# Attention beside an MLP on one core: the value product always runs beside the next quad's scores, across batches; the first MLP stage follows one quad behind; spare score banks serve two flushes

## Chip, cores and metric

The kernel runs on one core of a Trainium2 chip. The metric is the device time of one execution in microseconds (us), lower is better. Before the change it was 466.85 us (median of 3 runs, 465.77 to 469.23). Engine names are those of the profile: PE (TensorE), PEld (its weight loads), DVE (VectorE), ACT (ScalarE), POOL (GpSimd), SP (SyncE, which issues most DMAs).

## The reference

Attention with a forgetting gate over 8 batches, 8 heads, 576 positions and head size 64, then an MLP with tanh-GELU over the 4608 tokens (512 to 2048 to 512):

```python
def _attn_ref(q, k, v, f):
    scores = (1.0 / np.sqrt(D)) * np.matmul(q, k.transpose(0, 1, 3, 2))
    cum = np.cumsum(np.log(np.clip(f, 0.0001, 1.0)), axis=-1)
    decay = cum[:, :, :, None] - cum[:, :, None, :]
    scores = np.where(causal, -1000000000.0, scores + decay)
    ...                                    # softmax over the last axis
    return np.matmul(attn, v)

def _moe_ref(x, w_in, w_out):              # x: (B*S, H*D)
    h = x @ w_in
    return gelu_tanh(h) @ w_out
```

## The kernel before

Heads go in quads of four, two quads to a batch, 16 in all. For a quad:

- the scores come in four rounds, 48 matmuls with 32 rows each in all (8 or 16 a round); two ACT exponentials per round read them from two tiles of the score pool `psS` (two tiles of two PSUM banks each) and write `pt`;
- DVE multiplies the diagonal blocks of `pt` by a triangle, the **masks**; the strips are t = 0 to 4, and the last score round makes those of t = 2 and t = 4;
- the **value product** of one head is seven matmuls into `po` (two banks, a single buffer). Its columns 256 to 831 hold the numerators on one half of the partitions and the denominators on the other. An ACT copy (`num`) and a DVE transpose (`den`) read it. After two heads come a reciprocal, a second transpose (`rb`), and a **POOL multiply** that writes `xT`, the MLP's input;
- POOL also makes `v_aug`, the values times the gate's weight, the product's stationary operand.

The first MLP stage of a batch (`mlp_in`: 128 matmuls into `psS` tiles, 16 GELUs on ACT) needs `xT` of both quads. The second (`mlp_out`) is a generator: `pull(fill, n)` takes n of its 512-column matmuls as filler between other work.

```python
    def attn_out(i, h):                                   # value product of head h of quad i
        po = psO.tile([128, 1024], FP32, name="po", tag="po")
        p, va = pt[i % 2], v_aug[i % 2]
        for t in (0, 1, 3, 2, 4):
            for (a, z, base) in po_parts:
                ...                                       # matmuls into po
        ...
        nc.scalar.copy(num[mine, :], po[mine, 256:256 + S])
        nc.vector.transpose(out=den[mine, :], in_=po[other, 256:256 + S])
        if y == 1:                                        # second head of a pair
            ...                                           # rec = 1 / den; rb = rec, transposed
            nc.gpsimd.tensor_mul(xT[b % 2][:, 2 * u + x, :], num, rb)

    def step(i, j, fill, per_round, n=None):              # scores of quad i, products of quad j
        for r in range(4):
            if i is not None:
                score_round(i, r)
                ...
            if j is not None:
                attn_out(j, r)
            if r == 0:
                ...
                if i is not None:
                    make_vaug(i)
            ...                                           # r 1, 2: transposes of k, q of quad n
            if i is not None and r > 0:
                mask(i, r - 1)
            pull(fill, per_round)
            if i is not None and r == 3:
                mask(i, 3)

    # the loop over batches, from batch 1 on
            elif b + 1 < B:
                i = QPB * (b + 1)
                extra = b % 2
                pull(fill, 3)
                step(i, None, fill, 5 + 2 * extra)        # scores, no products
                step(i + 1, i, fill, 5 + extra)           # both
                step(None, i + 1, fill, 3)                # products, no scores: a flush
                pull(fill, 5)
```

The softmax here doesn't subtract the row's maximum and nothing guards it: scores larger than these inputs give would overflow.

Of the kernel before, what the change touches and what calls it, by code (L numbers as in the profile page):

```python
# [8 lines left out]
FP32 = mybir.dt.float32  # L9
# [7 lines left out]
def kernel(  # L17
# [10 lines left out]
    nc = tc.nc  # L28

    B, H, S, D = q.shape  # L30
# [10 lines left out]
    NQ = BH // 4  # L41
    QPB = H // 4
# [22 lines left out]
    psS = ctx.enter_context(tc.tile_pool(name="psS", bufs=2, space=bass.MemoryType.PSUM))  # L65
    psO = ctx.enter_context(tc.tile_pool(name="psO", bufs=1, space=bass.MemoryType.PSUM))
# [30 lines left out]
    def load_heads(src, dst, i, eng):  # L97
        b, h0 = i // QPB, 4 * (i % QPB)

        return [eng.dma_start(  # L100
            out=dst[i % 2][32 * h:32 * h + 32].rearrange("p a e d -> p a (e d)"),
            in_=src[b, h0 + h].rearrange("(a p e) d -> p a (e d)", p=32, e=2),
        ) for h in range(4)]

    def load_qk(i):
        return load_heads(k, k_nat, i, nc.sync) + load_heads(q, q_nat, i, nc.sync)
# [6 lines left out]
    def load_v(b, h0=0, nh=H):  # L113
        ins = []
        for t in range(NT):
            n = min(128, S - 128 * t)
            ins.append(nc.sync.dma_start(
                out=v_nat[b % 2][:n, t, h0:h0 + nh, :],
                in_=v[b, h0:h0 + nh, 128 * t:128 * t + n, :].rearrange("h p d -> p h d"),
            ))  # L120
        return ins
# [24 lines left out]
    def cast_k(i):  # L146
        nc.gpsimd.tensor_copy(k_bf, k_nat[i % 2])

    def cast_q(i):
        nc.gpsimd.tensor_copy(q_bf, q_nat[i % 2])  # L150

    def transpose_k(i):
        transpose_one(k_bf, kT[i % 2])
# [46 lines left out]

    pair = [None, None]

    def attn_out(i, h):
        po = psO.tile([128, 1024], FP32, name="po", tag="po")
        p, va = pt[i % 2], v_aug[i % 2]

        for t in (0, 1, 3, 2, 4):
            for (a, z, base) in po_parts:
                s = max(a, 128 * t)
                if s >= z:  # L210
                    continue
                nc.tensor.matmul(  # L212
                    po[:, base + s - a:base + z - a],
                    va[:, t, h, :],
                    p[:, h, strip_off[t] + s - 128 * t:strip_off[t] + z - 128 * t],
                    start=(t == 0), stop=(t == (1 if z == 256 else 4)),
                    skip_group_check=True,
                )
        b, u, x, y = i // QPB, i % QPB, h // 2, h % 2
        if y == 0:  # L220
            pair[0] = num_pool.tile([128, S], FP32, name="num", tag="num")
            pair[1] = den_pool.tile([128, S], FP32, name="den", tag="den")
        num, den = pair
        mine, other = slice(64 * y, 64 * y + 64), slice(64 - 64 * y, 128 - 64 * y)
        nc.scalar.copy(num[mine, :], po[mine, 256:256 + S])  # L225
        nc.vector.transpose(out=den[mine, :], in_=po[other, 256:256 + S])  # L226
        if y == 1:

            rec = den_pool.tile([128, S // 32], FP32, name="rec", tag="rec")
            nc.vector.reciprocal(rec, den[:, 0:S:32])  # L230
            rb = den_pool.tile([128, S], FP32, name="rb", tag="rb")
            nc.vector.transpose(out=rb.rearrange("p (c j) -> p c j", j=32),  # L232
                                in_=rec.unsqueeze(2).to_broadcast([128, S // 32, 32]))
            nc.gpsimd.tensor_mul(xT[b % 2][:, 2 * u + x, :], num, rb)  # L234


    def mlp_in(b, fts):

        hS = S // 2
        tiles = [psS.tile([128, 2, 512], FP32, name="ps_h", tag="s") for _ in fts]  # L240
        for dts in (range(N_DT - 1), range(N_DT - 1, N_DT)):
            for ft, ph in zip(fts, tiles):
                for dt in dts:
                    for j in range(2):
                        nc.tensor.matmul(  # L245
                            ph[:, j, 0:hS],
                            w_in_sb[:, dt, 128 * ft:128 * ft + 128],
                            xT[b % 2][:, dt, hS * j:hS * (j + 1)],
                            start=(dt == 0), stop=(dt == N_DT - 1),
                        )  # L250
        o = S * (b % 2)
        for ft, ph in zip(fts, tiles):
            nc.scalar.activation(  # L253
                gT[:, ft, o:o + S].rearrange("p (j n) -> p j n", j=2),
                ph[:, :, 0:hS], AF.Gelu_apprx_tanh)
# [63 lines left out]
    def make_w():  # L319
        cum_ps = psM.tile([128, NT * BH], FP32, name="cum_ps", tag="m")  # L320
        nc.tensor.matmul(cum_ps, utri_f32, logfT, start=True, stop=False)
        nc.tensor.matmul(cum_ps[:, BH:], ones_f32, before, start=False, stop=True)
        for (rows, t0, t1) in ((128, 0, NT - 1), (LAST, NT - 1, NT)):
            nc.scalar.activation(
                wT[:rows, :, t0:t1, :].rearrange("p i t h -> p t i h"),
                cum_ps[:rows, t0 * BH:t1 * BH].rearrange("p (t i h) -> p t i h", i=NQ, h=4),
                AF.Exp, scale=-1.0, bias=shift[:rows, :])


    def pull(it, n):  # L330
        for _ in range(n):
            if next(it, False) is False:
                return
# [4 lines left out]
    def step(i, j, fill, per_round, n=None):  # L338
# [5 lines that stand above are left out]
                if i == 0 and r == 0:  # L344
                    make_w()
            if j is not None:
                attn_out(j, r)
            if r == 0:
                if n is not None:
                    cast_k(n)  # L350
                    cast_q(n)
                if i == 0:
                    w_in_dmas.append(load_w_in(0))
                if i is not None:
                    make_vaug(i)
            if n is not None:
                if r == 1:
                    transpose_k(n)
                if r == 2:
                    transpose_q(n)  # L360
# [6 lines that stand above are left out]
    def prepare_one(i):  # L367
        cast_k(i)
        transpose_k(i)
        cast_q(i)  # L370
        transpose_q(i)

    def prepare(b):

        for i in range(b * QPB, b * QPB + QPB):
            prepare_one(i)
            if i + QPB < NQ:
                load_qk(i + QPB)
        if b + 1 < B:
            load_v(b + 1)  # L380

    with tc.manual_schedule():
        setup()
        step(0, None, none, 0, n=1)
        w_in_dmas.extend(load_w_in(c) for c in range(1, 4))
        qk2 = load_qk(2)
        after(qk2[0], w_in_dmas[2])
        step(1, 0, none, 0)
        w_out_dmas = [load_w_out(c) for c in range(2)]
        v1 = load_v(1)  # L390
        after(v1[0], w_out_dmas[0])
        load_qk(3)
        step(None, 1, none, 0)
        fill = none
        for b in range(B):
            mlp_in(b, (0, 1))
            for x in fill:
                pass
            if b == 0:
                prepare_one(2)  # L400
                for c in range(2, 4):
                    load_w_out(c)
            elif b + 1 < B:
                prepare(b + 1)
            for ft in range(2, N_FT):
                mlp_in(b, (ft,))
            fill = mlp_out(out_tiles(b))
            if b == 0:
                step(2, None, fill, 9, n=3)
                load_qk(4)  # L410
                step(3, 2, fill, 4)
                load_qk(5)
                load_v(2)
                step(None, 3, fill, 1)
                pull(fill, 4)
            elif b + 1 < B:
                i = QPB * (b + 1)
                extra = b % 2
                pull(fill, 3)
                step(i, None, fill, 5 + 2 * extra)  # L420
                step(i + 1, i, fill, 5 + extra)
                step(None, i + 1, fill, 3)
                pull(fill, 5)
        for x in fill:
            pass

# [1 line left out]
_INS = ['q', 'k', 'v', 'f', 'moe_w_in', 'moe_w_out']  # L428
# [26 lines left out]
```

## Time and profile before

The page of the kernel before, parts 1 and 2 (busy time as a share of the span; busy tenths in 40 equal slices):

```profile
PE 373.1 (80%) x2789; PEld 216.9 (47%) x2825; DVE 180.3 (39%) x295; ACT 244.5 (53%) x340; POOL 130.0 (28%) x127
PE   1654699858997799967998799967998699968996
```

No engine is full on average. The row of PE shows where: it reaches 9 in every batch, in the first MLP stage, and falls to 6 to 8 in between. Two batches as windows (start to end of the stretch, its length, busy time of each engine with the number of its instructions, granted PE clock, DMA share and rate):

```profile
core 0: us, PE busy (x) PEld busy (x) DVE busy (x) ACT busy (x) POOL busy (x), PEclk, DMA share, GB/s
219.10:272.60 53.50, 46.14 (x357) 26.85 (x361) 21.27 (x35) 30.44 (x43) 16.14 (x15) 0.97 0.44 92
272.60:324.70 52.10, 43.22 (x340) 25.57 (x344) 20.46 (x34) 29.92 (x42) 14.64 (x14) 0.97 0.41 89
```

A batch took 52 to 53.5 us, and PE stood still for 7 to 9 us of it. Who waited for whom (total us, times, longest):

```profile
DVE den L226 <- ACT num L225: 82.8, 61, 2.2
PE po L212 <- DVE den L226: 37.3, 50, 1.6
PE po L212 <- DVE pt_95 L198: 16.5, 16, 1.1
```

Products waited 37.3 us for the transpose that frees `po`, and the transpose waited for the copy. The timeline where the mixed step meets the flush (start, duration, engine, line, operation, count, and in brackets the idle time before it and what ended that):

```profile
360.76 0.78 DVE L232 STREAM_TRANSPOSE rb<-rec 128x576 f32<-128x576 f32 x1
361.46 2.13 DVE L198 TENSOR_TENSOR pt_95<-pt_95,utri 128x512 bf16<-128x512 bf16 x3
361.69 1.42 POOL L234 TENSOR_TENSOR xT_96<-num,rb 128x576 bf16<-128x576 f32 x1 [4.24 <-DVE rb L232]
361.90 0.43 PE L212 MATMUL po<-pt_95,v_aug_93 128*128 128x128 bf16 x3 [1.01 <-DVE pt_95 L198]
363.44 0.39 PE L212 MATMUL po<-pt_95,v_aug_93 128*128 128x320 bf16 x2 [1.11 <-DVE pt_95 L198]
...
363.93 0.63 ACT L225 COPY num<-po 64x576 f32<-64x576 f32 x1 [4.31 <-PE po L212]
364.59 0.78 DVE L226 STREAM_TRANSPOSE den<-po 64x576 f32<-64x576 f32 x1 [1.00 <-ACT num L225]
365.43 1.49 PE L212 MATMUL po<-pt_95,v_aug_93 128*128 128x256 bf16 x7 [0.31 <-DVE den L226]
```

In the flush a product, a copy and a transpose follow one another (363.44 to 365.37), and only then may the next product start.

### The profile page before, as it was taken

What the parts mean: (1) busy time and instruction counts of PE and PEld (TensorE: products, weight loads), DVE (VectorE), ACT (ScalarE), POOL (GpSimd) and SP (SyncE); (2) the same over time, 40 slices, a digit from 0 to 9 for tenths busy, and PEclk for the clock granted to TensorE, in tenths of its full rate; (3) what the DMA queues carried; (4) which work ended last, traced back from release to release, by engine and by line L of the source; (5) the groups of instructions that cost most, each with busy time, mean ns of one, the idle gap of its engine ahead of it and who ended that gap; (6) DMA issues with size and microseconds to landing.
All of it is one profiled execution on the core that took longest, in us unless ns stands there. A gap on an engine that the chain in (4) does not pass through costs nothing.

```text
span 465.6 us, 6954 instructions
## 1 busy us (share of the span) xinstructions
PE 373.1 (80%) x2789; PEld 216.9 (47%) x2825; DVE 180.3 (39%) x295; ACT 244.5 (53%) x340; POOL 130.0 (28%) x127
## 2 busy tenths in 40 slices
PE   1654699858997799967998799967998699968996
PEld 0222374425743465434734366434744366434752
DVE  5474412464127530455126530365215540364011
ACT  2733357714675347733676247743677247743610
POOL 1443380115502181024601272024601262022000
PEclk9999999967999899989999899999999899998999
DMA  9996980592941059000971049100961010000011
GB/s 189 146 193 111 201 146 24 124 196 63 227 94 45 24 127 200 24 23 34 207 134 47 23 108 210 34 24 24 226 125 46 2 44 1 24 23 23 24 46 68
DMA packets 86016, 42.55 MB, mean 91 GB/s; under 512 B 40352, under 2 KB 81312, under 8 KB 85984
## 3 DMA queue, kind: packets, MB, share of 16 engines
q1 hardware_dynamic: 79328, 36.73, 36.2%
q0 software_dynamic: 4224, 4.19, 5.8%
q10 hardware_dynamic: 2432, 1.18, 1.3%
q8 instruction: 22, 0.36, 0.3%
q14 instruction: 10, 0.08, 0.1%
HBM read 36.85 MB, written 9.44 MB: 99 GB/s over the span
## 4 chain that ended last, share of the span: by engine, by line
PE 53%; DVE 18%; ACT 15%; issue 6%; DMA 3%; POOL 2%; POOLq 0%; SPq 0%; ACTq 0%; DVEq 0%
PE ps_h L245 25%; PE pso L263 14%; PE po L212 10%; DVE den L226 9%; ACT num L225 7%; PE ps_s L180 4%; ACT pt_94 L189 4%; DVE pt_95 L198 3%; ACT pt_95 L189 3%; DVE rb L232 3%; DVE pt_94 L198 2%; POOL xT_96 L234 1%; DMA k_nat_82<-in_k_dram 1%; DMA k_nat_83<-in_k_dram 1%; DMA q_nat_81<-in_q_dram 1%
## 5 line engine op out<-in xcount | busy, mean ns | idle before, releaser
L263 PE MATMUL pso<-w_out_sb,gT 128*128 128x512 bf16 x540 | 140.2, 391 | 1.9 <-issue 0.6
L245 PEld LDWEIGHTS <-w_in_sb 128*128 128x128 bf16 x1024 | 101.7, 99 | 39.8 <-issue 10.5
L253 ACT ACTIVATE gT<-ps_h 128x576 bf16<-128x576 f32 x128 | 82.4, 650 | 66.9 <-PE ps_h L245 66.9
L225 ACT COPY num<-po 64x576 f32<-64x576 f32 x64 | 40.4, 632 | 93.8 <-PE po L212 93.3
L226 DVE STREAM_TRANSPOSE den<-po 64x576 f32<-64x576 f32 x64 | 49.9, 780 | 83.0 <-ACT num L225 82.8
L263 PEld LDWEIGHTS <-gT 128*128 128x128 bf16 x576 | 51.6, 100 | 57.5 <-issue 9.2
L212 PE MATMUL po<-pt_95,v_aug_93 128*128 128x320 bf16 (+4 forms) x224 | 39.0, 316 | 43.1 <-DVE den L226 26.5
L245 PE MATMUL ps_h<-xT_96,w_in_sb 128*128 128x288 bf16 x512 | 67.6, 293 | 5.0 <-POOL xT_96 L234 4.6
L245 PE MATMUL ps_h<-xT_97,w_in_sb 128*128 128x288 bf16 x512 | 65.4, 288 | 3.2 <-POOL xT_97 L234 3.2
L198 DVE TENSOR_TENSOR pt_94<-pt_94,utri 128x512 bf16<-128x512 bf16 (+1 forms) x40 | 21.8, 565 | 111.3 <-ACT pt_94 L189 110.9
L234 POOL TENSOR_TENSOR xT_97<-num,rb 128x576 bf16<-128x576 f32 x16 | 22.6, 1412 | 144.4 <-DVE rb L232 144.4
L234 POOL TENSOR_TENSOR xT_96<-num,rb 128x576 bf16<-128x576 f32 x16 | 22.6, 1410 | 129.5 <-DVE rb L232 119.0
L189 ACT ACTIVATE pt_95<-ps_s 128x800 bf16<-128x800 f32 (+3 forms) x64 | 50.1, 834 | 15.6 <-PE ps_s L180 15.2
L189 ACT ACTIVATE pt_94<-ps_s 128x800 bf16<-128x800 f32 (+3 forms) x64 | 50.1, 834 | 14.5 <-PE ps_s L180 14.4
L212 PEld LDWEIGHTS <-v_aug_93 128*128 128x128 bf16 x224 | 24.3, 115 | 65.0 <-issue 56.8
L267 DVE COPY o_st<-pso 128x512 f32<-128x512 f32 x36 | 24.8, 688 | 63.2 <-PE pso L263 62.9
L212 PE MATMUL po<-pt_94,v_aug_92 128*128 128x320 bf16 (+4 forms) x224 | 30.2, 276 | 15.9 <-DVE den L226 10.8
L180 PE MATMUL ps_s<-qT_88,kT_90 32*128 32x400 bf16 (+5 forms) x384 | 25.2, 295 | 12.2 <-ACT pt_94 L189 6.6
L212 PEld LDWEIGHTS <-v_aug_92 128*128 128x128 bf16 x224 | 20.1, 101 | 27.2 <-issue 20.4
L232 DVE STREAM_TRANSPOSE rb<-rec 128x576 f32<-128x576 f32 x32 | 24.9, 778 | 2.2
L180 PEld LDWEIGHTS <-kT_90 32*128 32x128 bf16 x384 | 10.1, 95 | 30.9 <-issue 24.8
L198 DVE TENSOR_TENSOR pt_95<-pt_95,utri 128x512 bf16<-128x512 bf16 (+1 forms) x40 | 23.1, 609 | 0.0
(55 smaller groups left out, 184.9 us busy)
## 6 DMA issues: line engine op xcount, KB each, us to landing
out_dram<-o_st SPq DMA_DIRECT2D x36, 256.0 KB, 2.0
k_nat_82<-in_k_dram SPq DMA_DIRECT2D x32, 144.0 KB, 3.1
k_nat_83<-in_k_dram SPq DMA_DIRECT2D x32, 144.0 KB, 4.4
v_nat_87<-in_v_dram SPq DMA_DIRECT2D x16, 256.0 KB, 5.8
q_nat_80<-in_q_dram SPq DMA_DIRECT2D x28, 144.0 KB, 3.8
q_nat_81<-in_q_dram SPq DMA_DIRECT2D x28, 144.0 KB, 5.0
v_nat_86<-in_v_dram SPq DMA_DIRECT2D x12, 256.0 KB, 5.9
w_in_sb<-in_moe_w_in_dram POOLq DMA_DIRECT2D x4, 512.0 KB, 6.3
```

The lines of the kernel that those rows point to most:

```text
L180: nc.tensor.matmul(tiles[h // 2][:, h % 2, c0:c0 + nq], kk[32 * h:32 * h + 32, 128 * t:128 * t + 128, c], qq[32 * h:32 * h + 32, q0:q0 + n ...
L189: nc.scalar.activation(p[:, 2 * g:2 * g + 2, off:off + n], tiles[g][:, :, 0:n], AF.Exp, scale=scale)
L198: nc.vector.tensor_mul(p[:, :, o:o + w], p[:, :, o:o + w], utri[:, :, :w].to_broadcast([128, 4, w]))
L212: nc.tensor.matmul(po[:, base + s - a:base + z - a], va[:, t, h, :], p[:, h, strip_off[t] + s - 128 * t:strip_off[t] + z - 128 * t], start ...
L225: nc.scalar.copy(num[mine, :], po[mine, 256:256 + S])
L226: nc.vector.transpose(out=den[mine, :], in_=po[other, 256:256 + S])
L232: nc.vector.transpose(out=rb.rearrange("p (c j) -> p c j", j=32), in_=rec.unsqueeze(2).to_broadcast([128, S // 32, 32]))
L234: nc.gpsimd.tensor_mul(xT[b % 2][:, 2 * u + x, :], num, rb)
L245: nc.tensor.matmul(ph[:, j, 0:hS], w_in_sb[:, dt, 128 * ft:128 * ft + 128], xT[b % 2][:, dt, hS * j:hS * (j + 1)], start=(dt == 0), stop=( ...
L253: nc.scalar.activation(gT[:, ft, o:o + S].rearrange("p (j n) -> p j n", j=2), ph[:, :, 0:hS], AF.Gelu_apprx_tanh)
L263: nc.tensor.matmul(pso, gT[:, ft, c:c + 128], w_out_sb[:, ft, :], start=(ft == 0), stop=(ft == N_FT - 1))
L267: nc.vector.tensor_copy(st, pso)
```

## The change

The intent is that, once the pipeline is filled, no product runs without scores beside it, and no scores without a product (quads 0 and 2 still make their scores alone). The pipeline of quads therefore runs on across batches. The first MLP stage of batch b starts when the products of its second quad are done, and by then the scores of the next batch's first quad are made already. Only quad 1 (nothing else to run yet) and the last quad still have a flush; there every second product goes to a bank pair of the score pool, which nothing else uses then. The transpose is put ahead of the copy.

```diff
-    def attn_out(i, h):
-        po = psO.tile([128, 1024], FP32, name="po", tag="po")
+    def attn_out(i, h, spare=False):
+        if spare:
+            po = psS.tile([128, 2, 512], FP32, name="ps_o", tag="s").rearrange("p a n -> p (a n)")
+        else:
+            po = psO.tile([128, 1024], FP32, name="po", tag="po")
...
+        nc.vector.transpose(out=den[mine, :], in_=po[other, 256:256 + S])
         nc.scalar.copy(num[mine, :], po[mine, 256:256 + S])
-        nc.vector.transpose(out=den[mine, :], in_=po[other, 256:256 + S])
...
-                attn_out(j, r)
+                attn_out(j, r, spare=(i is None and r % 2 == 1))
...                                    # batch 0: step(2, None, 7), step(3, 2, 4), step(4, 3, 3)
             elif b + 1 < B:
-                i = QPB * (b + 1)
-                extra = b % 2
+                i = 2 * b + 3
+                per_round = 7 + 2 * (b % 2)
                 pull(fill, 3)
-                step(i, None, fill, 5 + 2 * extra)
-                step(i + 1, i, fill, 5 + extra)
-                step(None, i + 1, fill, 3)
-                pull(fill, 5)
+                step(i, i - 1, fill, per_round)
+                if i + 1 < NQ:
+                    step(i + 1, i, fill, per_round)
+                else:
+                    step(None, i, fill, 5)
+                    pull(fill, 6)
```

Casts, transposes and loads of q, k and v move with the quads (cut here).

## The prediction

> **What bounds it now.** The page's first part shows PE busy 80% of 465.6 us, ACT 53%, DVE 39%. Stretches by stage show about 53 us per batch: 14 us of first MLP stage with PE full, then 38 us of attention filled with the second MLP stage, PE busy 28 to 31. The chain of waits ends 16% of the span in the DVE transpose and ACT copy of `po`. The timeline of one batch (338 to 378 us) splits the 38: four rounds with scores and filler but no value product, 9.5 us (2.4 each: the two exponentials take 1.5 to 1.7 and the next scores wait for them); four with both, 11.5 us; a flush of four without scores, 11.3 us, where each product (0.7 us of issue warm, 1.5 cold) waits for the copy (0.63) then transpose (0.78) of the one before. Value products waited 37 us in all for transposes.
>
> **The change, costed.** Matmul counts stay. Two full steps replace empty step, full step and flush in batches 1 to 5. From the mixed rounds: scores 0.51, product 0.69, six fillers 1.39 us (0.22 each plus 0.1 for switching). So a round with 7 fillers is about 2.82 us, with 9 about 3.28. ACT needs 2.3 of it (two exponentials, one copy), DVE under 2.5 on average: PE should bind. In rounds 1 and 3 of the old mixed step the product waited 0.4 to 0.6 us, since the copy stands behind two exponentials and the transpose behind the copy. Transposing first lets it run beside the exponentials; the pair still takes 1.4 us serially (the Trainium skill, PSUM — Partial Sum Buffer, "PSUM bank collisions raise a hardware error", has different quadrants harmless, but the trace shows every transpose after its copy), so a bare flush gains only by the spare banks.
>
> Steady batch: first stage with its tail 17.2 us (its wait for the last `xT` falls from 1.1 to under 0.5), steps 23.5 or 27.1: 41 and 44 us, not 53.
>
> **Sum (spans).**
> - Flush of quad 1 (42.6 to 52): products back to back, 5.5 us saved.
> - Batch 0: steps 10.2 + 9 + 9 us (the last two bound by ACT); first stage of batch 1 starts near 96, not 109.7, with quad 4's scores made.
> - Batches 1 to 5: 46 + 40.5 + 44.5 + 40.5 + 44.5 = 216, giving 312.
> - Batch 6: 29 to its step's end, flush 7.5, pull 1.4: 350.
> - Batch 7: 38.5 as before.
> That is 388, plus 1.5 (span to time), plus 3 for small waits: 393 us.
>
> PE's clock should gain: the Trainium skill (TensorE: Matmul & The Clock Gate, Part 1) has an idle array throttled to half clock; here flush products took 1.49 us against 0.86 in full rounds, and the granted clock was 0.83 to 0.96 in attention stages, 1.00 in the MLP stage.
>
> **What would show it.** Products waiting for transposes under 10 us; PE about 90% busy; rounds of 2.8 and 3.3 us; periods alternating 41 and 44; granted clock 0.98 or more.
>
> **What would make it wrong.** The copy, waiting for the transpose in ACT's queue, holds up the exponentials when DVE is late (masks take 0.38 to 0.71 us); rounds then stretch to 3.2 to 3.6. Earlier loads compete with `w_out` near 55 to 75 us. The last `xT` chain (3.6 us) may stand exposed at each batch.

## The result and the profile after

The kernel after took 406.39 us (median of 4 runs, 405.86 to 407.24), against 466.31 us for the kernel before (4 runs). The ratio is 0.8707, 95% interval 0.8665 to 0.8749. Ratios in this document are the mean time of one kernel's fast runs over that of the other's of the same rounds, so not quite the ratio of the medians quoted. So 60 us were saved where 73 were forecast: the time is 13 us above the 393 us of the prediction.

The same parts of the page, after:

```profile
PE 354.4 (88%) x2825; PEld 209.4 (52%) x2825; DVE 199.2 (49%) x295; ACT 244.2 (60%) x340; POOL 135.0 (33%) x127
PE   0546699959899899979999899979999999989996
```

PE does the same work in a shorter span and is now 88% busy. DVE's busy time **rose** from 180.3 to 199.2 us with the same 295 instructions. The masks, 80 of them, account for it: they took 44.9 us in the trace before and 65.7 us in the trace after. Two batches, with the columns as before:

```profile
195.40:241.00 45.60, 43.61 (x361) 25.94 (x360) 23.37 (x35) 30.18 (x43) 16.09 (x15) 1.00 0.48 107
241.00:284.20 43.20, 40.48 (x345) 24.50 (x344) 23.35 (x34) 30.23 (x43) 16.11 (x15) 1.00 0.53 107
```

A batch takes 45.6 and 43.2 us in place of 53.5 and 52.1. PE still stands still for 2 to 2.7 us of it. The waits:

```profile
DVE den L228 <- PE po L215: 124.2, 53, 13.7
PE po L215 <- DVE pt_95 L198: 14.1, 16, 1.1
PE po L215 <- ACT num L229: 5.9, 9, 1.6
```

The transpose now waits for the product itself, not for the copy. A product waits 5.9 us in all for what frees its bank (37.3 before). The wait for the masks `pt_95` hardly moved: 14.1 us for 16.5. It stands in one place per batch, the **joint** where the first step meets the second:

```profile
175.09 0.78 DVE L228 STREAM_TRANSPOSE den<-po 64x576 f32<-64x576 f32 x1 [1.64 <-PE po L215]
...
176.20 0.78 DVE L235 STREAM_TRANSPOSE rb<-rec 128x576 f32<-128x576 f32 x1
176.90 3.20 DVE L198 TENSOR_TENSOR pt_95<-pt_95,utri 128x512 bf16<-128x512 bf16 x3
176.96 0.81 PE L215 MATMUL po<-pt_95,v_aug_93 128*128 128x256 bf16 x5
...
177.12 1.43 POOL L237 TENSOR_TENSOR xT_97<-num,rb 128x576 bf16<-128x576 f32 x1 [4.13 <-DVE rb L235]
178.51 2.71 POOL L164 TENSOR_TENSOR v_aug_92<-v_nat_86,wT 128x640 bf16<-128x640 f32 x2
178.88 0.30 PE L215 MATMUL po<-pt_95,v_aug_93 128*128 128x320 bf16 x1 [1.11 <-DVE pt_95 L198]
180.15 0.19 PE L215 MATMUL po<-pt_95,v_aug_93 128*128 128x64 bf16 x1 [0.97 <-DVE pt_95 L198]
```

PE has the scores and five matmuls of the product behind it at 177.8 and then waits for two masks. The three masks at 176.90 take 0.38, 1.62 and 1.35 us. The second begins at 177.21, just after POOL's multiply began (177.12), and ends 0.28 us after it (178.83 after 178.55). The third stands against POOL's next instruction, the first half of `v_aug`, in the same way (180.10 after 179.95).

The Trainium skill (SBUF — State Buffer, "Who interferes with whom") states this: "A DVE instruction with two SBUF inputs contends with a GpSimd instruction that reads SBUF", and the one that comes second blocks. The trace agrees. A mask has two inputs in SBUF and takes 0.38 to 0.43 us where no POOL instruction runs beside it; the transposes of `po` have one input, in PSUM, and take 0.78 us with or without a POOL multiply beside them. Both pieces of POOL's work at the joint, the multiply into `xT` and `v_aug`, read SBUF.

The second of them was not at this place before. A `v_aug` buffer comes free when its quad's products end. Before, both buffers were free after the flush, and POOL made both during the MLP stage (in the trace before, at 328.5 and 331.1 us, far from any mask). After, one buffer still serves the running pipeline, and the second `v_aug` of a batch can only be made when the first step's products are done, which is the joint.

To count, here are the seven distances between the starts of the eight score rounds of a batch, for two batches, worked out from the start of each round's first score matmul in the trace. The fifth is the joint; the eighth round is not in it, since the MLP stage follows:

```
                    9 fillers a round                     7 fillers a round
predicted           3.28 in each                          2.82 in each
kernel after        3.35 3.17 3.24 3.18 5.30 3.17 3.24    2.92 2.92 2.81 2.75 5.29 2.74 2.81
```

Six of the seven distances lie within 0.11 us of the forecast. The joint costs 2.1 or 2.5 us more than the rounds beside it.

### The profile page after: what moved, and what is told of

Read it like the earlier page. It is cut to its first block, busy times and chain, and to the rows that moved or that the text cites. A ratio compares the mean times of both kernels' runs of the same rounds, so it can differ in the third digit from the quotient of the medians.

```text
span 404.6 us, 6926 instructions
## 1 busy us (share of the span) xinstructions
PE 354.4 (88%) x2825; PEld 209.4 (52%) x2825; DVE 199.2 (49%) x295; ACT 244.2 (60%) x340; POOL 135.0 (33%) x127
## 3 DMA queue, kind: packets, MB, share of 16 engines
q10 hardware_dynamic: 2432, 1.18, 1.4%
## 4 chain that ended last, share of the span: by engine, by line
PE 71%; DVE 17%; DMA 4%; POOL 3%; ACT 3%; issue 2%; SPq 0%; POOLq 0%; DVEq 0%; ACTq 0%
PE ps_h L248 29%; PE pso L266 25%; PE po L215 11%; PE ps_s L180 6%; DVE pt_95 L198 5%; DVE den L228 4%; DVE rb L235 3%; DVE pt_94 L198 3%; POOL xT_96 L237 1%; DMA q_nat_81<-in_q_dram 1%; DMA k_nat_82<-in_k_dram 1%; DMA k_nat_83<-in_k_dram 1%; DVE rec L233 1%; POOL xT_97 L237 1%; ACT pt_94 L189 1%
## 5 line engine op out<-in xcount | busy, mean ns | idle before, releaser
L266 PE MATMUL pso<-w_out_sb,gT 128*128 128x512 bf16 x576 | 138.4, 383 | 0.0
L248 PEld LDWEIGHTS <-w_in_sb 128*128 128x128 bf16 x1024 | 100.1, 98 | 35.6 <-issue 7.9
L228 DVE STREAM_TRANSPOSE den<-po 64x576 f32<-64x576 f32 x60 | 46.8, 781 | 124.5 <-PE po L215 124.2
L248 PE MATMUL ps_h<-xT_96,w_in_sb 128*128 128x288 bf16 x512 | 65.0, 286 | 3.3 <-POOL xT_96 L237 2.5
L248 PE MATMUL ps_h<-xT_97,w_in_sb 128*128 128x288 bf16 x512 | 64.5, 286 | 2.8 <-POOL xT_97 L237 2.8
L229 ACT COPY num<-po 64x576 f32<-64x576 f32 x60 | 37.9, 632 | 42.0 <-DVE den L228 34.6
L215 PE MATMUL po<-pt_95,v_aug_93 128*128 128x320 bf16 (+4 forms) x196 | 29.7, 281 | 16.2 <-DVE pt_95 L198 14.1
L215 PE MATMUL po<-pt_94,v_aug_92 128*128 128x320 bf16 (+4 forms) x224 | 30.6, 277 | 9.3 <-ACT num L229 3.9
L198 DVE TENSOR_TENSOR pt_94<-pt_94,utri 128x512 bf16<-128x512 bf16 (+1 forms) x40 | 36.8, 952 | 3.2 <-ACT pt_94 L189 3.2
L215 PEld LDWEIGHTS <-v_aug_93 128*128 128x128 bf16 x224 | 19.8, 104 | 24.5 <-issue 19.2
L215 PEld LDWEIGHTS <-v_aug_92 128*128 128x128 bf16 x224 | 19.2, 102 | 20.3 <-issue 13.8
L198 DVE TENSOR_TENSOR pt_95<-pt_95,utri 128x512 bf16<-128x512 bf16 (+1 forms) x40 | 28.8, 746 | 0.0
L180 PE MATMUL ps_s<-qT_88,kT_90 32*128 32x400 bf16 (+5 forms) x384 | 20.6, 300 | 8.1 <-DVE kT_90 L139 4.5
L180 PE MATMUL ps_s<-qT_89,kT_91 32*128 32x400 bf16 (+5 forms) x384 | 20.5, 295 | 1.2 <-DVE qT_89 L139 1.2
```

Of the source, the lines that this page charges most:

```text
L180: nc.tensor.matmul(tiles[h // 2][:, h % 2, c0:c0 + nq], kk[32 * h:32 * h + 32, 128 * t:128 * t + 128, c], qq[32 * h:32 * h + 32, q0:q0 + n ...
L198: nc.vector.tensor_mul(p[:, :, o:o + w], p[:, :, o:o + w], utri[:, :, :w].to_broadcast([128, 4, w]))
L215: nc.tensor.matmul(po[:, base + s - a:base + z - a], va[:, t, h, :], p[:, h, strip_off[t] + s - 128 * t:strip_off[t] + z - 128 * t], start ...
L248: nc.tensor.matmul(ph[:, j, 0:hS], w_in_sb[:, dt, 128 * ft:128 * ft + 128], xT[b % 2][:, dt, hS * j:hS * (j + 1)], start=(dt == 0), stop=( ...
L266: nc.tensor.matmul(pso, gT[:, ft, c:c + 128], w_out_sb[:, ft, :], start=(ft == 0), stop=(ft == N_FT - 1))
```

## The experiments

Eleven kernels were run, for three questions: which part of the change gave what; is POOL's work at the joint the cause of the missing 13 us; and what of it can be had back. All of them were timed in three rounds, the last combination in five.

| kernel | median us | range us | ratio to before, 95% interval |
|---|---|---|---|
| order alone, on before | 448.51 | 446.85 to 449.01 | 0.9605 (0.9573 to 0.9636) |
| spare banks alone, on before | 443.15 | 443.03 to 445.07 | 0.9506 (0.9474 to 0.9537) |
| schedule alone | 444.99 | 444.46 to 446.39 | 0.9517 (0.9472 to 0.9561) |
| after, old order | 437.78 | 436.14 to 439.15 | 0.9379 (0.9341 to 0.9418) |
| after, no spare banks | 412.63 | 411.02 to 414.36 | 0.8830 (0.8797 to 0.8863) |
| after | 406.39 | 405.86 to 407.24 | 0.8707 (0.8665 to 0.8749) |
| three `v_aug` | 400.11 | 399.75 to 400.18 | 0.8564 (0.8531 to 0.8596) |
| `v_aug` late | 398.44 | 397.39 to 399.19 | 0.8528 (0.8497 to 0.8559) |
| fillers first | 399.23 | 398.71 to 399.80 | 0.8547 (0.8519 to 0.8575) |
| POOL late | 394.10 | 392.61 to 396.33 | 0.8441 (0.8397 to 0.8485) |
| combined | 392.57 | 391.43 to 395.06 | 0.8398 (0.8367 to 0.8430) |
| no last mask (wrong result) | 384.78 | 384.55 to 385.14 | 0.8226 (0.8195 to 0.8258) |

### The parts of the change

**Order alone** (p1_order_only), on the kernel before:

```diff
+        nc.vector.transpose(out=den[mine, :], in_=po[other, 256:256 + S])
         nc.scalar.copy(num[mine, :], po[mine, 256:256 + S])
-        nc.vector.transpose(out=den[mine, :], in_=po[other, 256:256 + S])
```

> The kernel before with only the transpose put ahead of the copy. If the copy's place behind the exponentials is what made the mixed rounds' products wait 0.4 to 0.6 us, and the last xT chain is 0.6 us shorter: 456 to 461 us, products waiting for the pair under 30 us. Rival, that a copy held behind DVE in ACT's queue holds up the exponentials: 466 us or more.

It took 448.51 us, 18 us less. The direction was right, the size twice what was expected; the waits of products for the pair fell less than expected, to 31.1 us where under 30 was stated. Only the product's own wait and the last `xT` had been counted. In the traces, between the first MLP stages of batches 3 and 4, the second round of the mixed step fell from 3.00 to 2.52 us, the tail from the last product to the bulk of the MLP stage from 6.47 to 5.81 us, and, not counted, the first product of the flush from 3.38 to 2.68 us: with the transpose earlier, all of DVE's queue is earlier, and the masks that this product waits for stand in that queue. A further 0.65 us of the flush is the clock and not the order: its second product took 0.84 us in place of 1.49, and the granted clock from the last scores to the MLP stage was 1.00 in place of 0.90. The rival, a copy that holds up the exponentials, falls.

**Spare banks alone** (p2_spare_only), on the kernel before, in all eight flushes; the edit is the first and third hunk of the diff above.

> The kernel before with only the spare score banks in every flush (8 flushes instead of 2). A flush becomes bound by PE and the masks: 3 to 4 us less in each, 5 in quad 1's: about 438 us (432 to 446). If the flush is bound by something else (DVE's masks and transposes, cold clock): above 450.

It took 443.15 us, within the range: products waited 16.2 us for transposes in its trace, 37.3 before. The flush of the kernel before was bound mainly by the release of its one product bank pair.

**The change with the old order** (p3_old_order): the edit above, reversed, on the kernel after.

> The kernel after with copy first, transpose second, as it was. With 7 or 9 fillers a round covers most of the longer release, so only the end of each batch (0.6 us longer xT chain) shows: 408 to 412 us. Rival, that the new order is what costs the missing 13 us, by holding ACT: 400 us or less.

It took 437.78 us, 31 us more than the kernel after. Both stated outcomes missed, and the rival missed in the wrong direction. The argument that the fillers cover a late release holds for some products: the third round stays as it was (3.24 us with nine fillers). It does not hold for what stands behind the transpose in DVE's queue. The joint with the old order:

```profile
185.58 0.78 DVE L229 STREAM_TRANSPOSE den<-po 64x576 f32<-64x576 f32 x1 [1.61 <-ACT num L228]
...
186.47 0.42 PE L215 MATMUL po<-pt,v_aug 128*128 128x256 bf16 x2
...
187.40 3.20 DVE L198 TENSOR_TENSOR pt<-pt,utri 128x512 bf16<-128x512 bf16 x3
...
187.83 0.43 PE L215 MATMUL po<-pt,v_aug 128*128 128x128 bf16 x3 [0.94 <-DVE pt L198]
189.38 0.30 PE L215 MATMUL po<-pt,v_aug 128*128 128x320 bf16 x1 [1.11 <-DVE pt L198]
190.65 0.19 PE L215 MATMUL po<-pt,v_aug 128*128 128x64 bf16 x1 [0.97 <-DVE pt L198]
```

The fillers before it began at 184.40 in this trace and at 174.89 in that of the kernel after; from there the transpose starts 1.18 us later with the old order (185.58 less 184.40) and 0.20 us later with the new (175.09 less 174.89). Rec, `rb`, three masks and POOL's multiply all slip by about a microsecond, so that PE now waits for three masks in a row. Then the tail to the MLP stage is longer too (6.59 for 5.19 us), and the first round's release shows in the second (3.74 for 3.17). Some of the 31 us is a fallen clock: in batch 3 the nine fillers of the joint took 3.62 us at a granted clock of 0.62, and that joint lasted 8.2 us. But in batches 1 and 4, where the mean clock was 1.00 in both traces, the old order still costs 2.6 and 4.1 us a batch.

**The change without spare banks** (p4_no_spare): `attn_out(j, r)` in place of the call with `spare`.

> The kernel after without spare banks. Quad 1's flush takes 6 us more, the last flush 1.5 us more: 413 to 415 us. The rest of the trace unchanged.

It took 412.63 us, 6.2 us more than the kernel after, slightly less than expected. In the traces the first stage of batch 0 starts 5.6 us later (50.7 for 45.1) and batch 6 is 2.0 us longer (41.5 for 39.5), about as expected; batch 0 gives 1.0 us back (53.6 for 54.5). Batch 4 is 1.4 us longer in this profiled run, its slowest of four: the granted clock fell to 0.62 for 4 us there.

**The schedule alone** (p5_schedule_only): both of the last two edits.

> The kernel after with the old order of copy and transpose and without spare banks: the re-scheduling alone. If the parts add up (438 without the order, 6 more without the spare banks): 442 to 446 us. If order and spare banks overlap in what they hide: under 441.

It took 444.99 us: the parts of the change add up in this direction. So the new schedule by itself is worth 22 us of the 60, and the order of two reads is worth 18 us on the old schedule but 32 us on the new one (444.99 to 412.63), where the traces show more work waiting behind that transpose.

### The joint

**Three buffers of `v_aug`** (e1_three_vaug):

```diff
-    v_aug = many(2, [128, NT, 4, 128], BF16, "v_aug")
+    v_aug = many(3, [128, NT, 4, 128], BF16, "v_aug")      # and v_aug[i % 3], third one zeroed
...
-                step(i, i - 1, fill, per_round)
+                step(i, i - 1, fill, per_round, vaugs=(i, i + 1))
-                    step(i + 1, i, fill, per_round)
+                    step(i + 1, i, fill, per_round, vaugs=())   # and load_v ahead of prepare
```

> The kernel after with three v_aug buffers; from batch 1 on both quads' v_aug are made beside the first step, so POOL no longer builds one at the joint of the two steps; the multiply into xT stays there. If masks at the joint are slow (1.2 us for 0.4) because POOL reads SBUF beside them: the last masks fall to about 0.4, the joint's wait of 1.8 to 2.1 us to about 1, 400 to 402 us. Rival, that the masks are merely late behind exponentials and DVE's own queue: 406 us, unchanged.

It took 400.11 us, as expected of the theory. The last mask at the joint fell from 1.35 to 0.28 us; the one beside the multiply into `xT` stayed at 1.62 (1.02 in batches with nine fillers). The joint round fell from 5.30 to 4.23 us.

**`v_aug` late** (e2_vaug_late): no new buffer, `make_vaug(i)` of the second step moves from its first round to its third, behind the second round's multiply in POOL's queue.

> The kernel after with the second step's v_aug made in its third round, so behind the multiply of its second round in POOL's queue; no buffer added. Same theory as with three buffers, and batch 0's last step gains too: 398 to 402 us. Rival: 406 us.

It took 398.44 us, with the same joint round (4.23 us). Batch 0, which the three buffers had left alone, gained 1.2 us (53.3 for 54.5 us from one first MLP stage to the next).

**POOL late** (e5_pool_late): as before, and the multiply of the first step's last pair also waits until the second step's first multiply has been issued.

```diff
-            nc.gpsimd.tensor_mul(xT[b % 2][:, 2 * u + x, :], num, rb)
+            if defer and h == 3:
+                kept.append((xT[b % 2][:, 2 * u + x, :], num, rb))
+            else:
+                nc.gpsimd.tensor_mul(xT[b % 2][:, 2 * u + x, :], num, rb)
+                while kept:
+                    nc.gpsimd.tensor_mul(*kept.pop())
```

> As with the late v_aug, and the first step's last multiply into xT is also put behind the second step's first one, so POOL is idle at the joint. If POOL is the whole reason: masks there 0.38 to 0.43 us, the joint's wait under 0.4 us, 394 to 398 us. Rival (order and exponentials): at least 1 us of wait stays in each joint.

It took 394.10 us. The joint of its trace, with no POOL instruction in it:

```profile
174.88 0.78 DVE L237 STREAM_TRANSPOSE rb<-rec 128x576 f32<-128x576 f32 x1
175.58 0.92 DVE L198 TENSOR_TENSOR pt<-pt,utri 128x512 bf16<-128x512 bf16 x3
175.63 1.11 PE L217 MATMUL po<-pt,v_aug 128*128 128x256 bf16 x7
...
176.58 1.67 PE L273 MATMUL pso<-w_out_sb,gT 128*128 128x512 bf16 x7
```

The three masks take 0.92 us in place of 3.20, and the product's seven matmuls go through in 1.11 us where they took 3.38. The joint round is 3.01 us (2.8 elsewhere). The rival, that the masks were merely late behind exponentials and DVE's own queue, can account for no more than the 0.2 to 0.4 us that stay. One thing got worse: batch 1's stretch is 48.3 us for 47.6, since it takes 8.2 us from batch 0's last product to the bulk of the next stage, for 5.8. Of these 2.4 us only 0.7 are POOL's: the last multiply into `xT` now follows two multiplies and `v_aug` without a pause, and PE waits 2.23 us for it, for 1.50 (1.50 also with `v_aug` late alone). The rest is the clock: after this wait it was 0.57 for 3.4 us in the profiled run, and the eight fillers took 3.14 us for 1.89.

**Fillers first** (e3_fill_first): nothing is taken away from POOL; in the second step, of each round's fillers 7 or 9 (first round), 5 or 7, 2 and 0 go ahead of the product.

> The kernel after with the fillers of the joint round put ahead of its value product (7 or 9, then 5 or 7, 2 and 0 ahead in the four rounds; counts a round unchanged). The masks stay slow but PE has work meanwhile: 1.5 to 2 us less in each of 5 joints, 396 to 399 us. If the stall is only moved (to the next round's product, or to ACT): 404 us or more.

It took 399.23 us, just above the first outcome and well under the second. The masks stay slow, but PE has work meanwhile. With nine fillers the joint round falls to 3.36 us (the last one measured grows from 3.24 to 3.46); with seven, whose fillers last only 1.6 us, it is 3.78, and the following rounds grow to 3.22 and 3.02, so part of the stall only moves. A wait can be covered without removing its cause, but less well.

**No last mask** (e4_no_last_mask), wrong (relative error 0.73): the two masks of each quad's last round left out.

> A wrong result on purpose: the kernel after without the two masks of each quad's last score round (the multiplies stay on POOL where they were). It bounds what waiting for those masks costs. If they are the whole joint: joint rounds of 2.8 and 3.3 us, 391 to 395 us, so about what putting POOL's work later gave (394). If clearly under 390, there is more in the joint than POOL's share; if over 398, the gain of the late POOL work came from elsewhere.

It took 384.78 us, the outcome "clearly under 390". But the total is no clean bound of the joint: 32 masks are gone everywhere, also in batch 0 and in the setup, where they are slow too (the first stage of batch 0 starts at 41.9 us for 45.1). The stretches from batch 1 to batch 6 are the fair comparison. They sum to 214.1 us here, 226.8 in the kernel after, 218.8 with POOL late. In four of the five the first and the last differ by at most 0.8 us (40.4 44.0 40.4 44.0 against 40.5 44.8 40.5 44.8), so there nearly all of what these masks cost was POOL's doing. The fifth is batch 1, with the fallen clock of POOL late.

**Combined** (e6_combined): POOL late, with `v_aug` in the second round behind both multiplies, and 3, 2 and 1 fillers ahead of the product in the second step's first three rounds.

> Late POOL work, with v_aug made one round earlier (behind both multiplies, so that it no longer delays the last xT of the step), and 3, 2 and 1 fillers ahead of the value product in the second step's first three rounds. The remaining joint wait of 0.2 to 0.3 us and batch 1's longer xT tail (8.2 for 5.8 us) go: 389 to 393 us. If v_aug now delays the xT of the second round's successor or the masks of other rounds: 394 or more.

It took 392.57 us, the lowest time of a correct kernel here. The joint is gone (3.20 and 2.76 us in that round). The longer tail into batch 1 did not go: PE waits the same 2.23 us for the last `xT`. It takes 6.6 us for 8.2 because the clock stayed at 1.00 in this profiled run. Its advantage over POOL late is not settled: the intervals of the two ratios overlap. Against the kernel after it is about 3.5% less (0.8398 over 0.8707, so from two ratios to the same kernel and not from common rounds).

### What remains in batch 0

Batch 0's last two steps were predicted at 9 us each and took 11.5 and 13.8 (score starts at 74.39, 85.88 and the MLP stage at 99.67). The second has the joint with POOL: with POOL late its joint round is 2.80 us in place of 5.73. The first has another cause, in the trace after:

```profile
81.40 1.25 DVE L198 TENSOR_TENSOR pt_95<-pt_95,utri 128x512 bf16<-128x512 bf16 x1
...
82.68 0.78 DVE L228 STREAM_TRANSPOSE den<-po 64x576 f32<-64x576 f32 x1
...
83.55 0.63 ACT L229 COPY num<-po 64x576 f32<-64x576 f32 x1 [1.43 <-DVE den L228]
...
84.23 0.84 PE L215 MATMUL po<-pt_94,v_aug_92 128*128 128x256 bf16 x7 [1.55 <-ACT num L229]
```

DVE has a transpose of quad 4's keys and a slow mask in its queue, the transpose of `po` starts late, the copy waits for it, and the exponentials wait behind the copy. This looks like the danger that the prediction named for the new order, but the new order is not to blame: the round takes 3.82 us here and 3.76 with the old order. What is common is DVE's full queue. It was not tried alone.

## Why the prediction was right, and where it was 13 us short

- **What bounds the kernel, and that PE would bind after.** Right. PE went from 80% to 88% busy (about 90% forecast), products wait 5.9 us for their bank (under 10 forecast), and from batch 1 to 5 the rounds outside the joint last 2.74 to 2.92 and 3.17 to 3.35 us (2.82 and 3.28 forecast), but for one with a fallen clock.
- **Quad 1's flush, batches 6 and 7.** Right within 2 us: the first stage of batch 0 starts at 45.1 us (52.0 less 5.5 forecast, with 0.9 us of the rest already there before the first products); batch 7 took 38.7 us for 38.5. Batch 6 took 39.5 us for 37.9.
- **Batches 1 to 5: the term that was mis-sized.** "Batches 1 to 5: 46 + 40.5 + 44.5 + 40.5 + 44.5 = 216". Measured in the trace, from the start of one first MLP stage to the next: 47.56 + 44.32 + 46.05 + 42.77 + 46.05 = 226.75, so the periods forecast as 41 and 44 were 42.8 to 44.3 and 46.1. The step behind it is that all eight rounds of a batch are alike, in the form "steps 23.5 or 27.1": one round of the eight is the joint and costs 2.1 or 2.5 us more, about 11 us in five batches. With POOL moved out of the joint and a few fillers ahead (combined), the same five stretches are 46.19 + 40.37 + 44.72 + 40.37 + 44.71 = 216.36. So the schedule takes the time forecast for it once POOL's work no longer meets the masks at the joint.
- **Batch 0.** "steps 10.2 + 9 + 9" were 10.2 + 11.5 + 13.8 us. Part was made up by an earlier start, so batch 1's stage began at 99.7, not 96. The 13 us are, about: 3.7 here, 10.8 in batches 1 to 5, 1.6 in batch 6 and under 1 at the end, less the 3 us that the prediction had allowed for small waits.
- **What the prediction said could go wrong.** It had slow masks ("masks take 0.38 to 0.71 us") but read 0.71 as the mean of a merged line of three, when single masks took 1.62 us in that very trace; it had no thought for where POOL's `v_aug` would move; and it expected slow masks to act through the copy and ACT, when in steady batches they act on the product directly.
- **The order of transpose and copy.** Its mechanism was right, its size was not: the prediction gave it the rounds' 0.4 to 0.6 us, and the new schedule needs it for far more (32 us).
- **The clock.** Right in the steady part: of batches 1 to 6 five had a mean granted clock of 1.00 and batch 2 had 0.96. Over the whole run it was 0.952 in the profiled execution and 0.986 to 0.996 in the three others, where 0.98 or more was forecast. The Trainium skill (TensorE: Matmul & The Clock Gate, Part 1) has the array fall to half clock when it is not busy enough; in the profiled run the joint of batch 2 did that once, and cost a further 1.6 us against batch 4 (44.3 for 42.8):

```profile
170.00:176.00 6.00, 6.00 (x56) 2.96 (x55) 4.22 (x9) 4.64 (x8) 1.43 (x1) 1.00 0.13 46
176.00:180.40 4.40, 2.32 (x20) 0.87 (x19) 4.09 (x6) 2.10 (x3) 3.27 (x3) 1.00 0.00 0
180.40:184.50 4.10, 4.10 (x31) 1.91 (x30) 1.46 (x2) 1.88 (x3) 1.12 (x2) 0.58 0.17 64
```

  After the joint (176.0 to 180.4, PE busy 2.32 of 4.40 us) the granted clock was 0.58 for the next four microseconds.

Left open: whether copy and transpose could run at the same time. The Trainium skill (PSUM — Partial Sum Buffer, "PSUM bank collisions raise a hardware error") calls different 32-partition quadrants of a bank harmless, and the two read different halves of the partitions, but in every trace here, for one and the same product, one starts after the other has ended, and no run tried them together. That POOL's work makes the masks beside it slow is shown by the timing of single instructions and by three experiments that moved this work; that it is the shared port that blocks is the skill's statement, which the runs fit and do not prove.

## What to carry to other kernels

When a pipeline is made longer, a buffer comes free later, and the work that fills it moves: ask which engine does that work, what it will now run beside, and whether both read SBUF. Read the single instructions of a merged line before taking their mean as a cost, above all for an operation with two inputs in SBUF on DVE beside POOL. And what a release is worth is not only the next use of the buffer: everything that stands behind it in the same engine's queue moves with it. Before a longer stretch is put down to a change, look at its granted clock: here one fall cost about 1.7 us in the profiled run of POOL late, and the combined kernel had the same wait without it.

## What the Trainium skill lacked or had wrong

- SBUF — State Buffer, "Who interferes with whom": nothing wrong; the page gives no durations for such a pair, and the runs add them. A mask of 0.38 us became 1.02 to 1.62 us beside a POOL multiply of 1.43 us, and the smaller one of 0.28 us became 1.35 us beside `v_aug`; both ended 0.15 to 0.28 us after POOL's instruction. With two POOL instructions in a row, one mask got through at their boundary and the next one waited again.
- TensorE: Matmul & The Clock Gate, Part 1: its table gives the return to half clock "after ≥1 idle window (~3.4µs)". Read as one unbroken pause, that is too narrow for this case (elsewhere the page allows for short pauses, without saying how much of them). In the kernel after, 4.4 us with PE busy 2.32 us of them, and no gap longer than 1.11 us, were enough once (0.58 granted in the next 4.1 us); the same joint two batches later, with PE busy 1.92 us of 4.0, did not do it (1.00 in the next 4 us). Likewise a single wait of 2.23 us was followed by 3.4 us at 0.57 in POOL late and by a clock of 1.00 in the combined kernel.
